# A first weight load given as 100 and 28 partitions, and a residual added ahead of the last products

## The chip, the cores and the metric

The kernel runs on one core of a Trainium2 chip. The metric is the device time of one execution in microseconds; before the change it is 196.32 us, the median of three runs (196.27 to 196.67). The core has five engines that run their own instruction streams and meet at semaphores: TensorE (PE in the profile, its weight loads PEld), VectorE (DVE), ScalarE (ACT), GpSimd (POOL) and SyncE (SP), which here issues nearly all of the transfers. Sixteen DMA engines move the data.

## The reference

One decoding step for 8 sequences: a layer of cached attention over the last 2,048 of 8,192 positions, then an MLP, each with a layer norm ahead of it and a residual.

```python
def _A_ref(x, k_cache, v_cache, wq, wo):          # x: 8 x 1 x 512
    q = (x @ wq)                                  # 32 heads of 128, 8 heads in the caches
    k, v = the last W = 2048 positions of the caches, each head used 4 times
    p = softmax(q k^T * Dh ** -0.5)
    return (p v) @ wo

def _B_ref(x, w1, w2, w3, w4):
    ...                                           # hs, from shifted parts of h
    x1 = x + hs
    h2 = gelu(layernorm(x1) @ w3) @ w4            # 512 -> 1792 -> 512
    return x1 + h2

x = A_x
h = x + _A_ref(layernorm(x), ...)
h2 = h + _B_ref(layernorm(h), ...)
return h2
```

With one position per sequence (S = 1) the shifted parts g0 to g3 are zero, so hs is zero and w1 and w2 are not needed. The result is h + layernorm(h) + gelu(layernorm(layernorm(h)) @ w3) @ w4. In this text "h's part" is h + layernorm(h).

## The kernel before, in words

The caches and the weights are some 79 MB, and the kernel streams them through on-chip memory once. SP issues all of these loads in one fixed order (`dma(SP, ...)`, line 187): wq, then the k and v blocks of 2 MB each into `ring`, a ring of eight buffers, then wo in four loads, w3 in one, and w4 in four. A load into a ring buffer waits until the products that read its former content are done; the first w4 load has such a wait (`w_free[1]`), the others follow it on SP without one. Each of the four w4 loads has a semaphore of its own (`sem_w4[0]` to `[3]`), and a load raises its semaphore by 16.

`B_w4` is 1,792 x 512. The loads take rows 0 to 511, 512 to 1023, 1024 to 1535 and 1536 to 1791; partition p of a load gets r neighbouring rows (r = 4, 4, 4, 2), which are 4,096 bytes (2,048 in the last load) that lie together in memory. So the first load is 128 partitions of 4,096 bytes. All loads of the stream have 128 partitions; x (`x_sb`, loaded at the start from ACT's queue) and the result have 8.

The attention part fills most of the time: transposes of k (L283), their copies to on-chip memory (L292, L294), scores (L303), softmax, products with v (L373). Behind it comes the tail, written out in a fixed order on each engine:

- `oR` (L414, L419) reorders the heads, `pe_wo` (L426) multiplies by wo into `hT_ps`.
- VectorE and TensorE make the sums for the layer norms (L512 to L526), `uT` among them. ScalarE takes two roots, `s2` (L542) and `s1` (L543); VectorE's reciprocal of `s2` is `r2` (L544).
- `pe_w3` (L536): 56 products in two parts, of 8 and 6 columns of the result, into `y_ps`. They need `uT` and w3.
- For each part VectorE multiplies by `r2` into `g_x` (L554), and ScalarE applies the gelu into `gT` (L556).
- Behind these on VectorE stands h's part: the reciprocal `r1` of `s1` (L557), `xb` (L558, L559), `fin` (L560), and its split into two bf16 halves, `f_hi` (L561) and `f_lo` (L562). The event at its end is `e_fin`.
- `pe_w4` (L568 through the helper `rows`): the products of `gT` with w4, in four chunks that go with the four loads, 16, 16, 16 and 8 matmuls, all added up in `z_ps`. Between the third chunk and the fourth, `pe_fin` (also L568) adds `f_hi` and `f_lo` by products with an identity, 8 matmuls.
- VectorE and ScalarE copy the four parts of `z_ps` out (L597, L595), and SP stores the result (L600).

An engine takes its instructions in the order in which the code lists them, and waits at an instruction whose semaphores have not come far enough.

Of the kernel before, what the change touches and what calls it, by code (L numbers as in the profile page):

```python
# [8 lines left out]
ALU = mybir.AluOpType  # L9
AX = mybir.AxisListType  # L10

B = 8
# [10 lines left out]
FC = F // 128  # L23
KC = D // 128
# [43 lines left out]
def bass_sequential_preLN__sliding_block_cached__mixer_s_mlp__decode_kernel(  # L68
# [23 lines left out]
    with es:  # L92
# [7 lines left out]
        ident_b = sb([128, 128], dt.bfloat16, "ident_b")  # L100
# [24 lines left out]
        w4_sb = ring[:, W4S, 0:FC * D].rearrange("p (k n) -> p k n", k=FC)  # L125
# [17 lines left out]
        NH = KC * B  # L143
        hp = sb([128, NH], dt.float32, "hp")
# [6 lines left out]
        hc = sb([128, NH], dt.float32, "hc")  # L151
# [3 lines left out]
        s1 = sb([128, B], dt.float32, "s1")  # L155
        s2 = sb([128, B], dt.float32, "s2")
        r1 = sb([128, B], dt.float32, "r1")
        r2 = sb([128, B], dt.float32, "r2")
        xb = sb([128, NH], dt.float32, "xb")
        fin = sb([128, NH], dt.float32, "fin")  # L160
# [3 lines left out]
        f_hi = sb([128, NH], dt.bfloat16, "f_hi")  # L164
        f_lo = sb([128, NH], dt.bfloat16, "f_lo")
# [14 lines left out]
        sem_wo = [S(f"sem_wo{i}") for i in range(NWO)]  # L180
        sem_x, sem_wq, sem_w3, sem_out = (S(n) for n in ("sem_x", "sem_wq", "sem_w3", "sem_out"))
        sem_w4 = [S(f"sem_w4{i}") for i in range(4)]
        PE, AC, DV, PO, SP = (Engine(S(n)) for n in ("s_pe", "s_act", "s_dve", "s_pool", "s_sp"))

        def dma(eng, dst, src, sem, *waits):
            def f(e):
                e.dma_start(dst, src).then_inc(sem, 16)  # L187
            eng.op(f, *waits, inc=False)
# [16 lines left out]
        e = DV.op(lambda e: e.bn_stats(st6[:, :], x_sb[:, :]), X)  # L205
        e = DV.op(lambda e: e.bn_aggr(mv[:, :], st6[:, :]), e)
        e = AC.op(lambda e: e.activation(rstd[:, :], mv[:, 1:2], ACT.Sqrt, bias=eps1[0:B, :], scale=1.0), e, e_eps)
        e = DV.op(lambda e: e.reciprocal(rstd[:, :], rstd[:, :]), e)
# [23 lines left out]
        e = PE.op(pe_xT, e_xln, e_idb)  # L232
# [35 lines left out]
        e_sp, e_max, e_mT, e_neg, e_negps, e_negc, e_exp, e_PT, e_pT, e_lsel, e_Lb, e_rL, e_scale = ({} for _ in range(13))  # L268
        NG = NB * 8
        LAST = NB - 1  # L270
# [114 lines left out]
        v3 = lambda t: t.rearrange("p (n b) -> p n b", b=B)  # L385
        vr = lambda t: t.rearrange("p (n b) -> p b n", b=B)

        def bc(t):
            a = t[:, :]
            return bass.AP(tensor=a.tensor, offset=a.offset, ap=[a.ap[0], [0, KC], [1, B]])  # L390

        hT_ps = S_ps[0]
# [90 lines left out]
        for l in loads:  # L483
            what, b, j = l
            if what == "wo":
                n, qh = b, QH // NWO
# [3 lines left out]
            n = place[l]  # L490
# [6 lines left out]
        w_free = [taken[quads[n - NS]] for n in (len(quads), len(quads) + 1)]  # L497
# [4 lines left out]
        w4_ends = []  # L502
        for (f0, r), sem in zip(w4_rows, sem_w4):
            lo = len(w4_chunks)
            for i in range(r):
                w4_chunks[lo + i] = slice(f0 + i, f0 + 128 * r, r)
            dma(SP, w4_sb[:, lo:lo + r, :].rearrange("p r n -> p (r n)"),
                B_w4[f0:f0 + 128 * r, :].rearrange("(p r) n -> p (r n)", r=r), sem, w_free[1] if lo == 0 else None)
            w4_ends.append(lo + r)
        assert len(w4_chunks) == FC  # L510

# [14 lines left out]
        e_hc = DV.op(lambda e: e.scalar_tensor_tensor(v3(hc[:, :]), bc(msum), -1.0 / D, v3(hd[:, :]),  # L526
                                                      ALU.mult, ALU.add))
# [14 lines left out]
        e = AC.op(lambda e: e.activation(s2[:, :], vsum[:, :], ACT.Sqrt, bias=eps2[:, :], scale=(1.0 + EPS) / D), e_vs)  # L542
        e1 = AC.op(lambda e: e.activation(s1[:, :], vsum[:, :], ACT.Sqrt, bias=eps1[:, :], scale=1.0 / D))  # L543
        e_r2 = DV.op(lambda e: e.reciprocal(r2[:, :], s2[:, :]), e)  # L544

        def bcf(t, n):
            a = t[:, :]
            return bass.AP(tensor=a.tensor, offset=a.offset, ap=[a.ap[0], [0, n], [1, B]])

        e_gT = []  # L550
        for n in range(2):
            fn = (FH, FC - FH)[n]
            cs = slice(n * FH * B, (n * FH + fn) * B)
            e = DV.op(lambda e, n=n, cs=cs, fn=fn: e.tensor_tensor(v3(g_x[:, cs]), v3(y_ps[n][:, 0:fn * B]), bcf(r2, fn),  # L554
                                                                   ALU.mult), e_y[n], e_r2)
            e_gT.append(AC.op(lambda e, cs=cs: e.activation(gT[:, cs], g_x[:, cs], ACT.Gelu_apprx_tanh), e))  # L556
        e = DV.op(lambda e: e.reciprocal(r1[:, :], s1[:, :]), e1)  # L557
        e = DV.op(lambda e: e.tensor_tensor(v3(xb[:, :]), v3(hc[:, :]), bc(r1), ALU.mult), e, e_hc)  # L558
        e = DV.op(lambda e: e.tensor_tensor(xb[:, :], xb[:, :], hp[:, :], ALU.add), e)  # L559
        e = DV.op(lambda e: e.tensor_tensor(fin[:, :], hT_ps[:, 0:NH], xb[:, :], ALU.add), e)  # L560
        e = DV.op(lambda e: e.tensor_copy(f_hi[:, :], fin[:, :]), e)  # L561
        e_fin = DV.op(lambda e: e.tensor_tensor(f_lo[:, :], fin[:, :], f_hi[:, :], ALU.subtract), e)  # L562

        z_ps = S_ps[1]

        def rows(e, w, rhs, start=False, stop=False):
            for nb in range(KC):
                ins = e.matmul(z_ps[32 * nb:32 * nb + B, 0:128], w[nb], rhs[nb], start=start, stop=stop,  # L568
                               tile_position=(0, 32 * nb), skip_group_check=True)
            return ins  # L570

        def pe_w4(lo, hi, *waits):
            def f(e):
                for fc in range(lo, hi):
                    ins = rows(e, [gT[:, fc * B:(fc + 1) * B]] * KC,
                               [w4_sb[:, fc, nb * 128:(nb + 1) * 128] for nb in range(KC)],
                               start=(fc == 0), stop=(fc == FC - 1))
                return ins
            return PE.op(f, *waits)

        def pe_fin(e):
            for part in (f_hi, f_lo):
                ins = rows(e, [part[:, nb * B:(nb + 1) * B] for nb in range(KC)], [ident_b[:, :]] * KC)
            return ins

        pe_w4(0, w4_ends[0], (sem_w4[0], 16), e_gT[0], e_exp[LAST])
        pe_w4(w4_ends[0], w4_ends[1], (sem_w4[1], 16))
        pe_w4(w4_ends[1], w4_ends[2], (sem_w4[2], 16), e_gT[1])
        PE.op(pe_fin, e_fin)
        e_z = pe_w4(w4_ends[2], w4_ends[3], (sem_w4[3], 16))  # L590
        zr, orow = [z_ps[32 * nb:32 * nb + B, 0:128] for nb in range(KC)], [out_sb[:, nb * 128:(nb + 1) * 128] for nb in range(KC)]
        e_out = []
# [45 lines left out]
```

## Time and profile before

| | before |
|---|---|
| time, median of three runs | 196.32 us |
| time of the profiled execution | 196.32 us |
| its span, first to last instruction | 194.5 us |
| TensorE busy (matmul) | 150.1 us, 77% |
| VectorE, ScalarE, GpSimd busy | 85.0, 79.9, 32.4 us |
| DMA | 79.57 MB, mean 409 GB/s |
| mean granted TensorE clock | 0.877; 0.50 from 175 us to the end |

The span is the time from the first to the last instruction that the profiler records; the execution is 1.8 us longer. "Busy" is the time of recorded instructions. In the views that follow, L and a number is a line of the kernel before, "<-" names what an engine waited for, and all times are microseconds from the start of the span unless they are marked ns.

### The profile page before, as it was taken

The numbers are of one execution on the slowest core, as the hardware profiler recorded it, in microseconds if no ns is written. First come the engines' busy times: TensorE is split into PE (matmuls) and PEld (weight loads), VectorE is DVE, ScalarE is ACT, GpSimd is POOL, SyncE is SP. The second block draws the span as 40 slices with busy tenths as digits, with TensorE's granted clock in tenths as the row PEclk, the third lists the DMA queues.
The fourth block names the chain that finished last, engine by engine and source line by source line (L and its number), as shares of the span: only waits on it lengthen the run. The fifth ranks groups of instructions, "written<-read, shape, count | busy, mean of one in ns | idle before, by whom it ended". The sixth has DMA issues, their size and how long they took to land.

```text
span 194.5 us, 6261 instructions
## 1 busy us (share of the span) xinstructions
PE 150.1 (77%) x2885; PEld 124.1 (64%) x2885; DVE 85.0 (44%) x209; ACT 79.9 (41%) x93; POOL 32.4 (17%) x39
## 2 busy tenths in 40 slices
PE   0027999978979992999579987998799893784563
PEld 0027877757758881888368866786678673684451
DVE  7501446556565443355415451545354536401033
ACT  5000577875845650456225642564454313000041
POOL 8000000070340250008000610071008000000000
PEclk9999999999999999699969997899999965555555
DMA  6999999999999999999999999999999999999970
GB/s 217 431 431 428 431 431 428 424 431 430 428 431 428 428 428 431 431 428 423 428 428 431 428 428 431 424 428 428 424 431 424 428 428 426 416 418 415 415 306 37
DMA packets 7001, 79.57 MB, mean 409 GB/s; under 512 B 688, under 2 KB 704, under 8 KB 2752
## 3 DMA queue, kind: packets, MB, share of 16 engines
q1 hardware_dynamic: 6960, 79.18, 96.2%
q8 instruction: 22, 0.36, 0.7%
q10 hardware_dynamic: 16, 0.01, 0.0%
q14 instruction: 3, 0.02, 0.0%
HBM read 79.18 MB, written 0.01 MB: 407 GB/s over the span
## 4 chain that ended last, share of the span: by engine, by line
DMA 57%; PE 35%; DVE 4%; SPq 1%; issue 1%; ACT 0%; DVEq 0%
DMA ring<-in_A_k_cache_dram 49%; PE kT_ps L283 16%; PE oT_ps L373 9%; DMA ring<-in_B_w_dram 8%; PE S_ps L303 5%; PE sm L348 2%; DVE P_sb L338 1%; DVE pT_sb L353 1%; SPq L187 1%; PE sm L361 1%; PE sm L326 1%; PE sm L316 1%; PE S_ps L568 1%; ACT P_sb L330 0%; DVE kT_sb L294 0%
## 5 line engine op out<-in xcount | busy, mean ns | idle before, releaser
L292 ACT ACTIVATE kT_sb<-kT_ps 128x1024 bf16<-128x1024 bf16 x64 | 65.4, 1024 | 73.2 <-PE kT_ps L283 72.6
L283 PE MATMUL kT_ps<-ident_p,ring 128*128 128x128 bf16 x1024 | 73.0, 229 | 12.5 <-DMA ring<-in_A_k_cache_dram 12.5
L283 PEld LDWEIGHTS kT_ps<-ident_p,ring 128*128 128x128 bf16 x1024 | 62.0, 103 | 26.7 <-DMA ring<-in_A_k_cache_dram 13.4
L294 DVE COPY kT_sb<-kT_ps 128x1024 bf16<-128x1024 bf16 x64 | 44.3, 692 | 66.4 <-PE kT_ps L283 66.4
L338 POOL TENSOR_TENSOR P_sb<-P_sb,mask_b 128x512 bf16<-128x512 bf16 x28 | 28.3, 1041 | 117.1 <-PE kT_ps L283 83.1
L373 PE MATMUL oT_ps<-pT_sb,ring 128*128 128x16 bf16 x1024 | 34.1, 172 | 3.9 <-DVE oT_all L382 3.9
L373 PEld LDWEIGHTS oT_ps<-pT_sb,ring 128*128 128x128 bf16 x1024 | 32.1, 100 | 6.1 <-issue 6.0
L303 PE MATMUL S_ps<-kT_sb,qwin 128*32 128x512 bf16 x256 | 27.0, 406 | 0.0
L353 DVE COPY pT_sb<-sm 128x512 bf16<-128x512 bf16 x32 | 13.4, 419 | 7.5 <-PE sm L348 7.5
L348 PE MATMUL sm<-ident_b,P_sb 128*128 128x128 bf16 x128 | 13.2, 230 | 3.9 <-DVE pT_sb L353 1.6
L348 PEld LDWEIGHTS sm<-ident_b,P_sb 128*128 128x128 bf16 x128 | 8.6, 101 | 6.2 <-issue 4.5
L542 ACT ACTIVATE s<-vsum,eps 128x8 f32<-128x8 f32 x1 | 0.3, 301 | 24.3 <-DVE vsum L525 24.3
L330 ACT ACTIVATE P_sb<-S_ps,negcol 128x512 bf16<-128x512 f32 x8 | 5.5, 688 | 7.8 <-DVE negcol L329 7.8
L303 PEld LDWEIGHTS S_ps<-kT_sb,qwin 128*32 128x32 bf16 x256 | 6.8, 93 | 3.0 <-issue 0.2
L238 PE MATMUL S_ps<-xlnT,wbig 128*128 128x8 bf16 x128 | 3.6, 168 | 5.2 <-DMA wbig<-in_A_wq_dram 5.2
L238 PEld LDWEIGHTS S_ps<-xlnT,wbig 128*128 128x128 bf16 x128 | 3.5, 104 | 5.2 <-issue 5.2
L227 PE MATMUL sm<-ident_b,xln_b 8*128 8x8 bf16 x4 | 0.3, 176 | 7.7 <-DVE xln_b L209 7.7
L312 DVE TENSOR_REDUCE mcol<-S_ps 128x1 f32<-128x512 f32 x8 | 5.5, 689 | 1.6 <-PE S_ps L303 1.5
L426 PE MATMUL S_ps<-oR,wbig 128*128 128x8 bf16 x128 | 4.0, 168 | 2.7 <-DMA wbig<-in_A_wo_dram 1.9
L426 PEld LDWEIGHTS S_ps<-oR,wbig 128*128 128x128 bf16 x128 | 3.7, 104 | 3.0 <-DMA wbig<-in_A_wo_dram 2.0
L227 PEld LDWEIGHTS sm<-ident_b,xln_b 8*128 8x128 bf16 x4 | 0.2, 118 | 7.7 <-DVE xln_b L209 7.7
L361 PE MATMUL sm<-lsel,ones_f 128*128 128x32 f32 x16 | 3.6, 314 | 1.3 <-DVE lsel L357 1.3
(87 smaller groups left out, 69.5 us busy)
## 6 DMA issues: line engine op xcount, KB each, us to landing
ring<-in_A_k_cache_dram SPq DMA_DIRECT2D x16, 2048.0 KB, 26.9
ring<-in_A_v_cache_dram SPq DMA_DIRECT2D x16, 2048.0 KB, 22.3
wbig<-in_A_wq_dram SPq DMA_DIRECT2D x1, 4096.0 KB, 12.3
wbig<-in_A_wo_dram SPq DMA_DIRECT2D x4, 1024.0 KB, 28.0
ring<-in_B_w_dram SPq DMA_DIRECT2D x1, 1792.0 KB, 27.0
ring<-in_B_w_dram SPq DMA_DIRECT2D x3, 512.0 KB, 15.4
ring<-in_B_w_dram SPq DMA_DIRECT2D x1, 256.0 KB, 15.2
x_sb<-in_A_x_dram ACTq DMA_DIRECT2D x1, 8.0 KB
```

What stands on the lines that cost most here:

```text
L238: ins = e.matmul(S_ps[0][:, h * B:(h + 1) * B], wq_v[:, kc, h * DH:(h + 1) * DH], xlnT[:, kc * B:(kc + 1) * B], start=(kc == 0), stop=(kc ...
L283: ins = e.matmul(kT_ps[i % 2][:, c * 128:(c + 1) * 128], ring[:, s, n * DH:(n + 1) * DH], ident_p[:, :], is_transpose=True)
L292: e_lo[i] = AC.op(lambda e: e.activation(kT_sb[:, i % NKT, 0:1024], kT_ps[i % 2][:, 0:1024], ACT.Copy), e_Tlo[i], e_QK.get(i - NKT))
L294: e_hi[i] = DV.op(lambda e: e.tensor_copy(kT_sb[:, i % NKT, 1024:2048], kT_ps[i % 2][:, 1024:2048]), e_Thi[i], e_QK.get(i - NKT))
L303: ins = e.matmul(S_ps[b % 2][32 * h:32 * (h + 1), :], qwin[:, b, 4 * j + h, w0:w0 + 32], kT_sb[:, i % NKT, :].rearrange("p (c h k) -> p h ...
L312: e_max[b] = DV.op(lambda e: e.tensor_reduce(mcol[:, :], S_ps[b % 2][:, :], AX.X, ALU.max), e_QK[8 * b + 7], e_mT.get(b - 1))
L338: e_sp[b, r] = eng.op(lambda e, r=r, pb=pb, mb=mb: e.tensor_tensor(P4_sb[:, 128 * r:128 * (r + 1), :], pb, mb, ALU.mult), e_exp[b], e_PT.g ...
L348: ins = e.matmul(pT_ps[:, x * 128:(x + 1) * 128], P4_sb[:, 32 * c:32 * (c + 1), :].rearrange("p k h -> p (k h)"), ident_b[:, :], is_transp ...
L353: e_pT[b, r] = DV.op(lambda e: e.tensor_copy(pT_sb[:, b % NB3, 4 * r:4 * (r + 1), :].rearrange("p c n -> p (c n)"), pT_ps[:, :]), e_PT[b, ...
L361: e_Lb[b] = PE.op(lambda e: e.matmul(sm[:, LB], ones_f[:, :], lsel[:, :], start=True, stop=True), e_lsel[b], e_pT[b, 3])
L373: ins = e.matmul(dst, ring[:, s, n * DH:(n + 1) * DH], pT_sb[:, b % NB3, c, :].rearrange("p (h c j r) -> p c j h r", h=4, c=4, j=2)[:, cq, j],
L426: ins = e.matmul(hT_ps[:, nb * B:(nb + 1) * B], wo_v[:, q, r, nb * 128:(nb + 1) * 128], oR[:, r, q * B:(q + 1) * B], start=(q == 0 and r = ...
```

## The change

The change has two parts.

The first w4 load becomes two loads on SP, one right after the other: partitions 0 to 99 (rows 0 to 399 of `B_w4`) and partitions 100 to 127 (rows 400 to 511). Every partition gets the same bytes as before. Both raise `sem_w4[0]`, so the first chunk of w4's products waits for 32 there. The description given with the change says of the split that lower-numbered DMA engines carry more of the load. The wait for the ring buffer stands on the first of the two.

h's part moves forward on two engines. On VectorE its six instructions stand right behind `r2`, ahead of both `g_x`. On TensorE its eight products come directly behind w3's and start the sum in `z_ps` (they carry `start`); the four chunks of w4 follow one another, and the last ends the sum. The number of products and of VectorE instructions is the same as before. The lines from the first insertion on have higher numbers in the changed kernel (L554 becomes L565, L557 to L562 become L550 to L555, L568 becomes L572).

```diff
+        P0 = 100
...
-            dma(SP, w4_sb[:, lo:lo + r, :].rearrange("p r n -> p (r n)"),
-                B_w4[f0:f0 + 128 * r, :].rearrange("(p r) n -> p (r n)", r=r), sem, w_free[1] if lo == 0 else None)
+            cuts = (0, P0, 128) if lo == 0 else (0, 128)
+            for p0, p1 in zip(cuts, cuts[1:]):
+                dma(SP, w4_sb[p0:p1, lo:lo + r, :].rearrange("p r n -> p (r n)"),
+                    B_w4[f0 + p0 * r:f0 + p1 * r, :].rearrange("(p r) n -> p (r n)", r=r), sem,
+                    w_free[1] if lo + p0 == 0 else None)
...
         e_r2 = DV.op(lambda e: e.reciprocal(r2[:, :], s2[:, :]), e)
+        e = DV.op(lambda e: e.reciprocal(r1[:, :], s1[:, :]), e1)
+        e = DV.op(... xb = hc * r1)
+        e = DV.op(... xb = xb + hp)
+        e = DV.op(... fin = hT_ps + xb)
+        e = DV.op(... f_hi = fin)
+        e_fin = DV.op(... f_lo = fin - f_hi)
...
-        (the same six lines, behind the loop over g_x and gT)
...
-                               start=(fc == 0), stop=(fc == FC - 1))
+                               stop=(fc == FC - 1))
...
-                ins = rows(e, [part[...] for nb in range(KC)], [ident_b[:, :]] * KC)
+                ins = rows(e, [part[...] for nb in range(KC)], [ident_b[:, :]] * KC,
+                           start=(part is f_hi))
...
-        pe_w4(0, w4_ends[0], (sem_w4[0], 16), e_gT[0], e_exp[LAST])
+        PE.op(pe_fin, e_fin, e_exp[LAST])
+        pe_w4(0, w4_ends[0], (sem_w4[0], 32), e_gT[0])
         pe_w4(w4_ends[0], w4_ends[1], (sem_w4[1], 16))
         pe_w4(w4_ends[1], w4_ends[2], (sem_w4[2], 16), e_gT[1])
-        PE.op(pe_fin, e_fin)
         e_z = pe_w4(w4_ends[2], w4_ends[3], (sem_w4[3], 16))
```

More of the change, by code (lines that the diff above doesn't have):

```diff
@@ L544, in bass_sequential_preLN__sliding_block_cached__mixer_s_mlp__decode_kernel @@
         e_r2 = DV.op(lambda e: e.reciprocal(r2[:, :], s2[:, :]), e)
+        e = DV.op(lambda e: e.reciprocal(r1[:, :], s1[:, :]), e1)
+        e = DV.op(lambda e: e.tensor_tensor(v3(xb[:, :]), v3(hc[:, :]), bc(r1), ALU.mult), e, e_hc)
+        e = DV.op(lambda e: e.tensor_tensor(xb[:, :], xb[:, :], hp[:, :], ALU.add), e)
+        e = DV.op(lambda e: e.tensor_tensor(fin[:, :], hT_ps[:, 0:NH], xb[:, :], ALU.add), e)
+        e = DV.op(lambda e: e.tensor_copy(f_hi[:, :], fin[:, :]), e)
+        e_fin = DV.op(lambda e: e.tensor_tensor(f_lo[:, :], fin[:, :], f_hi[:, :], ALU.subtract), e)
         def bcf(t, n):
@@ L556, in bass_sequential_preLN__sliding_block_cached__mixer_s_mlp__decode_kernel @@
             e_gT.append(AC.op(lambda e, cs=cs: e.activation(gT[:, cs], g_x[:, cs], ACT.Gelu_apprx_tanh), e))
[L557 to L562, printed above, removed]
         z_ps = S_ps[1]
@@ L582, in pe_fin @@
             for part in (f_hi, f_lo):
-                ins = rows(e, [part[:, nb * B:(nb + 1) * B] for nb in range(KC)], [ident_b[:, :]] * KC)
-            return ins
-        pe_w4(0, w4_ends[0], (sem_w4[0], 16), e_gT[0], e_exp[LAST])
+                ins = rows(e, [part[:, nb * B:(nb + 1) * B] for nb in range(KC)], [ident_b[:, :]] * KC,
+                           start=(part is f_hi))
+            return ins
+        PE.op(pe_fin, e_fin, e_exp[LAST])
+        pe_w4(0, w4_ends[0], (sem_w4[0], 32), e_gT[0])
         pe_w4(w4_ends[0], w4_ends[1], (sem_w4[1], 16))
         pe_w4(w4_ends[1], w4_ends[2], (sem_w4[2], 16), e_gT[1])
-        PE.op(pe_fin, e_fin)
         e_z = pe_w4(w4_ends[2], w4_ends[3], (sem_w4[3], 16))
```

## The prediction

> **What bounds the kernel now.** First the chain of waits from 184 us to the end, because both edits lie there. Its columns are start, duration and what the end waited for.
>
> ```profile
> 175.54 15.42 DMA ring<-in_B_w_dram
> 190.96 0.04 issue
> 191.00 1.05 PE S_ps L568 x32
> ...
> 192.08 0.28 DVE out_sb L597
> ```
>
> The end hangs on the weight loads, then on the last products of w4 (L568), then on the copy out. So an edit pays only as far as it brings forward the last landing of w4 or shortens the products behind it.
>
> Second, the activity by stretches of half a microsecond. The last two columns are the share of the 16 DMA engines that is busy and GB/s.
>
> ```profile
> 186.00:186.50 0.50, 0.00 (x0) 0.00 (x0) 0.39 (x3) 0.14 (x1) 0.00 (x0) 0.50 1.02 412
> 187.00:187.50 0.50, 0.15 (x5) 0.18 (x6) 0.00 (x0) 0.50 (x1) 0.00 (x0) 0.50 0.66 270
> 189.00:189.50 0.50, 0.50 (x23) 0.48 (x24) 0.17 (x2) 0.10 (x1) 0.00 (x0) 0.50 0.51 205
> 190.50:191.00 0.50, 0.00 (x0) 0.00 (x0) 0.24 (x2) 0.00 (x0) 0.00 (x0) 0.50 0.32 123
> ```
>
> Until 186.5 all engines move rows; at 187.2 two thirds do, at 189.2 half, at 190.7 five of sixteen. Every load gives every engine the same number of rows, yet the engines do not finish together. The sixteen increments that the last w4 load leaves in the trace say how far apart they are: six at 186.95 to 187.23, one each at 187.88 and 188.75, three at 189.89 to 190.11, five at 191.24 to 191.59. The kernel waits for these five.
>
> Third, what sets them back: the DMA queues (packets, MB, share of 16 engines).
>
> ```profile
> q1 hardware_dynamic: 6960, 79.18, 96.2%
> q8 instruction: 22, 0.36, 0.7%
> ```
>
> The 22 instruction fetches of 16 KB run on the same engines. On one engine the packet records follow each other without a gap (the next starts some 4 ns before the last one's recorded end), so the records can be strung into sixteen chains. The fetch at 18.55 us took 0.94 us, and the row behind it 1.10 us in place of 0.61, so its engine lost 0.93 + 0.49 = 1.42 us for good. The chains show the fetches going round eight engines in turn: 22 = 8 + 8 + 6, the last (189.6 us) too late to hold up more than an increment. So five engines lose three fetches (187.1 + 4.26 = 191.4, found 191.24 to 191.59) and three lose two (187.1 + 2.84 = 189.9, found 189.89 to 190.11).
>
> Which five? The load of x_sb has 8 partitions, 8 packets, and 8 of the chains carry one; I take these for the lower-numbered half. Where two chains run within 3 ns of each other they can be swapped, but by the best fit the turn goes over six engines of the upper half, then two of the lower, and the late five are the first five. If a turn goes over consecutive numbers upwards, that is 10 to 15, then 0 and 1, and the late five are 10 to 14. The trace has no engine numbers, and this step is the weakest.
>
> Last, the timeline behind w3's landing (187.21), which says what TensorE and VectorE must do meanwhile.
>
> ```profile
> 186.70 0.20 DVE L544 RECIPROCAL r<-s 128x8 f32<-128x8 f32 x1 [0.28 <-ACT s L542]
> 187.35 1.95 PE L536 MATMUL kT_ps<-uT,ring 128*128 128x8 bf16 x56 [1.72 <-DMA ring<-in_B_w_dram]
> 188.58 0.23 DVE L554 TENSOR_TENSOR g_x<-kT_ps,r 128x64 f32<-128x64 f32 x1 [1.68 <-PE kT_ps L536]
> 189.22 0.33 PEld L568 LDWEIGHTS S_ps<-ring,gT 128*8 128x8 bf16 x16
> 189.45 0.19 DVE L557 RECIPROCAL r<-s 128x8 f32<-128x8 f32 x1
> 190.58 0.19 DVE L562 TENSOR_TENSOR f_lo<-fin,f_hi 128x32 bf16<-128x32 f32 x1
> 191.00 0.60 PE L568 MATMUL S_ps<-ring,gT 128*8 128x128 bf16 x16 [0.70 <-DMA ring<-in_B_w_dram]
> 191.39 0.32 PE L568 MATMUL S_ps<-ident_b,f_hi 128*8 128x128 bf16 x4
> 191.63 0.40 PE L568 MATMUL S_ps<-ring,gT 128*8 128x128 bf16 x8
> ```
>
> VectorE idles 1.68 us while w3's products run; TensorE idles from about 190.3 to 191.0 for the third w4 load.
>
> **The split load.** A w4 row of 4,096 bytes follows the last after 155 ns on an engine (the first increments of the first two loads, 183.81 and 185.07, are 1.26 us apart for 8 rows and an increment). The loads seen share rows equally: 128 partitions as 8 rows on each of 16 engines, 8 as one row on each of 8. An equal share of 100 over at most 16 engines means 10 engines with 10 rows, of 28 it means 14 with 2. If the lower-numbered are taken, as the change says, engines 0 to 9 carry 12 rows in place of 8, 10 to 13 carry 2, and 14 and 15 none. [...]
>
> The sum for each group, by its last increment: engines 10 to 13, 191.24 to 191.59 less 6 x 0.155 = 0.93, so 190.31 to 190.66. Engine 14: less 1.24, at most 190.35. Engine 15: about 188.9. Engines 0 and 1: 189.90 plus 4 x 0.155 = 0.62, so 190.52. The rest: at most 188.75 + 0.62 = 189.37. The last landing moves from 191.59 to about 190.66, 0.93 us earlier. The third load moves as much, 190.96 to 190.03. w3 stands ahead of w4 in each engine's queue and stays at 187.21.
>
> The cost of issuing: one DMA more on SP, 0.47 to 0.60 us by the shorter issues of the trace. Behind it stand the other w4 loads and, much later, the store. SP finishes issuing at 179.07, and no engine's first w4 load ends before 183.81, so this hides; without that cover it would be those 0.5 us. The first wait of w4's products asks for 32 in place of 16, so for both parts: with the numbers above it is met at 187.5, before they can start.
>
> Unknown is whether rows in blocks of ten per engine are as fast as the old share. The nearest row is the store, 8 partitions at once: its 1,024-byte packets took 44 to 91 ns. So a row may cost anything from 155 ns to about twice that; below 155 ns no row has been seen. I take 155, since the three kinds of load with 128 partitions all run at one even rate, and keep the other end.
>
> **h's part.** Six VectorE instructions (L557 to L562, 189.45 to 190.77, 1.32 us) move ahead of g_x. They can start when r2 is done (186.90; s1 is ready at 186.85) and end at 188.22, and g_x starts at 188.58 when w3's first products are out: hidden with 0.36 us to spare. Without that cover, the first gelu and all w4 products would wait up to 1.32 us. On TensorE eight products (191.39 to 191.63, 0.24 us) move from the third gap between w4's chunks to behind w3's. There they delay w4's first products from 189.22 to 189.46. Sixteen products take 0.39 us (191.00 to 191.39), so three chunks end at 189.46 + 1.17 = 190.63, and the last chunk waits for its load until 190.66 + 0.04 = 190.70. Nothing is queued on TensorE behind these eight but w4. Left in place, they would start when f_lo is ready, 190.81, and end at 191.05: the move is worth 0.35 of the gain, and nothing without the earlier loads.
>
> **Sum.** The last chunk starts at 190.70 in place of 191.63, 0.93 us earlier; the tail behind it (copies, store) is unchanged. The profiled execution took 196.32 us with a span of 194.5, and 196.32 is also the median of the three runs: 196.32 - 0.93 = 195.39. More than 1.0 us is not to be had, since TensorE is then the bound (190.63).
>
> **Rivals.**
> *A late engine is among the ten (slower).* If the turn runs downwards, or starts elsewhere in another execution, one of the late engines carries 12 rows: 191.24 to 191.59 plus 0.62, so 0.27 to 0.62 us longer, 196.6 to 196.9. It decides as soon as one engine with three fetches is below 10. For it: no numbers in the trace, and 8 and 9 are of the upper half too. Against: six turns in the upper half and then two in the lower fit an upward count that wraps after 15. 15%.
> *Rows in blocks of ten are slow.* Doubled, the ten rows cost 1.55 us more on engines 0 and 1: 190.52 + 1.55 = 192.07, 0.5 us longer, 196.8. It eats gain from 0.14 us on and makes the kernel slower from 1.07 us. For it: the store's 91 ns. Against: these two engines run nearly 3 us behind most of the others, which have then left the same stretch. 11%: 3 in 100 still faster (about 195.8), 3 the same, 5 slower.
> *The parts go over all sixteen engines evenly, so nothing moves.* Then the five stay at 191.59, h's products have left a gap in which TensorE waits anyway, and the time is 196.3. [...] Against it: 100 has no equal share over 16. 6%.
>
> **How the numbers follow.** The forecast, 195.39 with its own range 195.2 to 195.7 (gain 1.0 at most and the 0.05 by which the runs go below the median; at the other end a third of a microsecond lost to slower rows or increments), has 68%. Below 195.2 TensorE forbids. With the partly slow rows and the even split, 195.2 to 196.5 holds 68 + 6 + 6 = 80%; the slower cases, 196.6 to 196.9, are left out. A measurement here can tell 0.2%, 0.39 us, from no change: faster 0.68 + 0.03 = 0.71, same 0.03 + 0.06 = 0.09, slower 0.15 + 0.05 = 0.20.
>
> **What would show it.** Right: five late increments near 190.3 to 190.66 with two more beside them; the DMA share still above 0.5 at 189.5 and near zero at 190.7; xb to f_lo between 186.9 and 188.3; h's products before w4's; the wait ahead of the last chunk nearly gone. Wrong: a last increment past 191.6 (a late engine was given more), g_x later than 188.6, or a first load that ends after 189.4.

## The result and the profile after

The changed kernel takes 199.56 us, median of six runs (199.06 to 200.39), against 196.68 us for the kernel before in the runs beside it (six runs, 196.27 to 198.98). The ratio is 1.0146, with a 95% interval of 1.0115 to 1.0176: 2.9 us slower, where 0.93 us less was forecast. The profiled execution took 199.06 us with a span of 197.3.

The chain of waits from 184 us on (start, duration, what the end waited for; "issue" is time for which the profile shows no wait):

```profile
184.00 0.35 PE S_ps L427 x13
184.35 4.04 issue
188.39 0.23 PE S_ps L427 x2
...
189.79 0.19 DVE uT L523
...
192.71 0.40 ACT gT L567 x2
...
193.11 1.69 PE S_ps L572 x44
...
194.83 0.28 DVE out_sb L602
```

The chain no longer names a weight load, but this reading is close to a tie. `uT` was ready at 189.98, and the last increment of w3's load came at 190.23; w3's products began at 190.36, which is 0.13 us after the landing, as before (187.21 and 187.35). The chain follows one of two nearly equal causes. The activity by stretches shows the other (last two columns: share of the DMA engines busy, GB/s):

```profile
183.00:183.50 0.50, 0.50 (x25) 0.50 (x23) 0.00 (x0) 0.00 (x0) 0.00 (x0) 0.50 1.12 258
186.00:186.50 0.50, 0.00 (x0) 0.00 (x0) 0.00 (x0) 0.00 (x0) 0.00 (x0) 0.50 0.98 291
187.00:187.50 0.50, 0.00 (x0) 0.00 (x0) 0.00 (x0) 0.00 (x0) 0.00 (x0) 0.50 0.91 268
189.00:189.50 0.50, 0.50 (x3) 0.50 (x4) 0.06 (x1) 0.00 (x0) 0.00 (x0) 0.50 1.01 215
193.00:193.50 0.50, 0.39 (x18) 0.42 (x22) 0.00 (x0) 0.10 (x1) 0.00 (x0) 0.50 0.13 49
```

The kernel before, in the same stretch:

```profile
183.00:184.00 1.00, 0.84 (x30) 0.76 (x29) 0.00 (x0) 0.00 (x0) 0.00 (x0) 0.50 1.03 414
```

The first of the five lines is the one to look for: at 183 us all engines are busy and move 258 GB/s, where the kernel before moved 414 with all engines busy. The engines are not idle, they are slow. The packet records say it row by row: w3's rows of 3,584 bytes take 140 ns until 182 us and a median of 250 to 284 ns between 183 and 185; rows of 4,096 bytes take a median of 159 ns until 183 us and of 268 to 334 between 183 and 186, 216 to 274 up to 190. From 191 on they take 159 again. In the kernel before no w4 row of 4,096 bytes took more than 159 ns, and of w3's 512 rows three took more than 140, one behind the other right after an instruction fetch. The slow stretch begins when the first engines reach the cut load (w3's first increment came at 182.69, the first slow row began at 182.84), and it covers engines that are still at w3, whose increments run on to 190.23.

The first cut load raised its semaphore by 24 single increments and two early ones, which fits 10 engines for the 100 partitions and 14 for the 28, as forecast. The rest did not follow:

| us | before | after |
|---|---|---|
| last increment of w3 | 187.21 | 190.23 |
| w3's products begin | 187.35 | 190.36 |
| last increments of the four w4 loads | 188.42, 189.66, 190.96, 191.59 | 191.26, 192.25, 193.47, 194.09 |
| the copies out begin | 192.08 | 194.83 |

The timeline of the tail:

```profile
190.36 1.95 PE L540 MATMUL kT_ps<-uT,ring 128*128 128x8 bf16 x56 [0.41 <-DVE msq L526]
191.21 1.28 ACT L567 ACT_TABLE_LOAD   x1
192.35 0.19 DVE L555 TENSOR_TENSOR f_lo<-fin,f_hi 128x32 bf16<-128x32 f32 x1
192.46 0.33 DVE L565 TENSOR_TENSOR g_x<-kT_ps,r 128x64 f32<-128x64 f32 x2
192.71 0.39 ACT L567 ACTIVATE gT<-g_x 128x64 bf16<-128x64 f32 x2 [0.22 <-DVE g_x L565]
193.11 1.66 PE L572 MATMUL S_ps<-ring,gT 128*8 128x128 bf16 x56
```

The cover for h's part is gone too: g_x comes right behind f_lo, not behind w3's first products. It costs little, since ScalarE's table load ends at 192.49 and the gelu starts at 192.71: 0.22 us.

### The profile page after: what moved, and what is told of

It is laid out like the page before. It is cut to its first block, busy times and chain, and to the rows that moved or that the text cites. A ratio compares the mean times of both kernels' runs of the same rounds, so it can differ in the third digit from the quotient of the medians.

```text
span 197.3 us, 6262 instructions
## 1 busy us (share of the span) xinstructions
PE 150.7 (76%) x2885; PEld 125.1 (63%) x2885; DVE 84.8 (43%) x209; ACT 79.7 (40%) x93; POOL 32.3 (16%) x39
## 4 chain that ended last, share of the span: by engine, by line
DMA 49%; PE 39%; DVE 6%; issue 4%; ACT 1%; SPq 0%; DVEq 0%
DMA ring<-in_A_k_cache_dram 49%; PE kT_ps L284 17%; PE oT_ps L374 9%; PE S_ps L304 5%; PE sm L349 2%; PE S_ps L427 2%; DVE P_sb L339 1%; DVE pT_sb L354 1%; PE sm L362 1%; PE S_ps L572 1%; PE sm L327 1%; PE sm L317 1%; DVE oT_all L383 0%; SPq L188 0%; ACT P_sb L331 0%
## 5 line engine op out<-in xcount | busy, mean ns | idle before, releaser
L284 PE MATMUL kT_ps<-ident_p,ring 128*128 128x128 bf16 x1024 | 73.9, 230 | 14.0 <-DMA ring<-in_A_k_cache_dram 14.0
L284 PEld LDWEIGHTS kT_ps<-ident_p,ring 128*128 128x128 bf16 x1024 | 62.8, 103 | 28.7 <-DMA ring<-in_A_k_cache_dram 15.0
```

What stands on the lines that cost most here:

```text
L284: ins = e.matmul(kT_ps[i % 2][:, c * 128:(c + 1) * 128], ring[:, s, n * DH:(n + 1) * DH], ident_p[:, :], is_transpose=True)
```

## The experiments

Three theories stood at the start, guesses of the author that the runs were to decide between. *Path*: in a load of 128 partitions every engine writes partitions that no other engine writes; in a load of fewer neighbouring partitions engines share the way to the same partitions, and everything that goes there slows. *Late engine*: only the number of rows on the engines that are behind counts. *Move*: h's part ahead of g_x is the loss. Ratios are to the kernel before, run beside each experiment, with 95% intervals.

**The cut alone.**

```diff
 # the kernel before, with
+            cuts = (0, 100, 128) if lo == 0 else (0, 128)
 # and 32 in the first chunk's wait
```

> The load as 100 and 28 partitions, h's part left in its old place. Path theory (the 100-partition load makes the DMA engines' rows slow for all): rows of 4,096 bytes take 230 to 330 ns in place of 159 from the first row of this load on, the last w4 increment lands near 194, and the time is 198.5 to 200, as with the whole change. Late-engine theory (only the number of rows on the late engines counts): rows stay at 159 ns, last increment at 191.9 to 192.3, time 196.7 to 197.3. Move theory (the slower time comes from h's part ahead of g_x): no loss, 196.3 to 196.7.

Measured: 199.55 us, ratio 1.0151 (1.0124 to 1.0177). Last w4 increment 195.08. This trace also settles the tie. Here `uT` was ready at 187.45 and TensorE still waited for w3's rows, which landed at 189.96:

```profile
190.09 1.94 PE L539 MATMUL kT_ps<-uT,ring 128*128 128x8 bf16 x56 [2.67 <-DMA ring<-in_B_w_dram]
```

The chain of waits of this trace, from 182 us on, names the weight loads up to 194.47:

```profile
177.51 16.96 DMA ring<-in_B_w_dram
194.47 0.04 issue
194.52 1.05 PE S_ps L571 x32
```

The cut by itself is the whole loss, and the late landings are how it acts. The long stall of TensorE in the profile after is not needed for it: here the stall at the same place is 1.55 us.

**The move alone.**

```diff
 # the changed kernel, with
-            cuts = (0, P0, 128) if lo == 0 else (0, 128)
+            cuts = (0, 128)
 # and 16 in the first chunk's wait
```

> One first load of 128 partitions, h's part moved. Path theory: rows at 159 ns, last increment at 191.6 as before, and the time within 0.2 us of before. Move theory: g_x late by up to 0.9 us and the time 197 to 199.5.

Measured: 196.44 us, ratio 0.9994 (0.9976 to 1.0012); last increment 191.45, rows at 159 ns. No difference that can be told. The move theory falls. In this execution g_x was again held by h's part:

```profile
187.68 1.98 PE L540 MATMUL kT_ps<-uT,ring 128*128 128x8 bf16 x56
188.85 1.28 ACT L567 ACT_TABLE_LOAD   x1
190.00 0.19 DVE L555 TENSOR_TENSOR f_lo<-fin,f_hi 128x32 bf16<-128x32 f32 x1
190.11 0.33 DVE L565 TENSOR_TENSOR g_x<-kT_ps,r 128x64 f32<-128x64 f32 x2
190.36 0.39 ACT L567 ACTIVATE gT<-g_x 128x64 bf16<-128x64 f32 x2 [0.23 <-DVE g_x L565]
```

The table load ends at 190.13, so the gelu lost 0.23 us.

**A cut with equal shares, 96 and 32, and one of 64 and 64.** Both are the changed kernel with another P0.

```diff
-        P0 = 100
+        P0 = 96      # and, in the other kernel, 64
```

> Cuts at 96 in place of 100: both parts can be shared equally by sixteen engines (6 and 2 rows each), so every engine keeps 8 rows, but no engine's block of rows is one of the old ones. Path theory, if the blocks are at fault: rows above 200 ns while the 96-partition part runs and the last increment later than 192; time 197.5 to 200. Late-engine theory (unequal numbers are at fault): rows at 159 ns, last increment 191.6, time as before.

> Cuts at 64: 4 rows on each engine from either part. If a block of four neighbouring partitions is what suits the engines, rows stay at 159 ns or nearly so, last increment 191.6, time as before. If any load of fewer than 128 partitions disturbs, rows above 200 ns and a time over 197.5.

Measured: 198.97 us, ratio 1.0127 (1.0101 to 1.0153), and 199.77 us, ratio 1.0154 (1.0128 to 1.0181). The first load raised its semaphore by 32 single increments in either, 16 for each part, so every engine has its 8 rows; and both lose about as much as the cut at 100. The late-engine theory falls as the cause. So does the guess that blocks of four neighbouring partitions suit the engines. The activity of the 64 and 64 kernel:

```profile
183.00:184.00 1.00, 0.73 (x28) 0.65 (x25) 0.00 (x0) 0.00 (x0) 0.00 (x0) 0.50 1.07 249
184.00:185.00 1.00, 0.00 (x0) 0.00 (x0) 0.00 (x0) 0.00 (x0) 0.00 (x0) 0.50 0.99 268
```

Two sequels were open: that any second load on the semaphore disturbs, or that it is the smaller number of partitions.

**Two loads, cut by columns.**

```diff
+            halves = 2 if lo == 0 else 1
+            c = r * D // halves
+            for j in range(halves):
+                dma(SP, w4_sb[:, lo:lo + r, :]...[:, j * c:(j + 1) * c], ...)   # all 128 partitions
```

> The first w4 load as two loads again, but cut by columns: each has all 128 partitions and half of their bytes. Path theory (in a load of 128 partitions every engine writes partitions that no other engine writes; a load of fewer makes engines share the way to the same partitions): rows of 2,048 bytes at 84 ns, rows of 4,096 at 159, last increment at 191.6 to 191.7, time within 0.3 us of before. Rival (two loads on one semaphore, or simply one load more in the queue, is what disturbs): rows slow as in the other cuts, time over 198.

Measured: 196.34 us, ratio 0.9991 (0.9975 to 1.0008); rows of 2,048 bytes at 84 ns and of 4,096 at 159, last increment 191.63.

```profile
183.00:184.00 1.00, 0.89 (x30) 0.81 (x30) 0.00 (x0) 0.00 (x0) 0.00 (x0) 0.50 1.04 410
184.00:185.00 1.00, 0.00 (x0) 0.00 (x0) 0.00 (x0) 0.00 (x0) 0.00 (x0) 0.50 1.03 408
```

One load more, and one semaphore for two, cost nothing that can be told. It is the cut by partitions.

**Half the first load, in one piece or in eight.** The upper 64 partitions of the first load are left out in both. The lower 64 come by one load, or by eight loads of 8 partitions with a step of 4.

```diff
+            parts = [slice(0, 64)] if lo == 0 else [slice(0, 128)]
 # or
+            parts = [slice(b + o, b + 32, 4) for b in (0, 32) for o in range(4)] if lo == 0 else [slice(0, 128)]
+            for j, ps in enumerate(parts):
+                dma(SP, w4_sb[ps, lo:lo + r, :]..., B_w4[...][ps, :], sem, ...)
 # and 16, or 128, in the first chunk's wait
```

> The upper 64 partitions of the first w4 load are left out; the lower 64 come by one load, 4 rows on each of 16 engines. Path theory: sixteen engines write where only eight wrote before, so rows slow to 230 ns and more while this load runs, though it moves half as many bytes; w3's last increment later than 188.5. Source theory (reading the weights' rows is what clashes): the same for this one.

> [...] Path theory: every row stays at 159 ns (140 for w3), w3's last increment at 187.2 as before. Source theory, or a cost of any load under 128 partitions: rows over 200 ns again.

Measured, one run each, so the rows count here and not the times: 197.56 us in one piece, 195.73 in eight. In one piece w4's rows between 183 and 184 us had a median of 216 ns, somewhat less than the 230 that was expected, w3's 196 with a longest of 296, and w3's last increment came at 188.64. In eight pieces the rows stayed at 159 and 140 (but for one beside a fetch), last increment of w4 190.62. The source theory falls with these. w3's last increment came at 187.55, 0.34 after that of before (187.21). The eight loads did not set it back: the last increment of the third wo load, before any row of w4 moved, was already 0.40 late (180.73 against 180.33).

The step of 4 was the author's choice under the path theory, meant to keep each engine to partitions of its own. No trace shows that it does so, and no other step was tried. What the runs show is the rows: 159 ns against 216 in this pair, 159 against 302 in the next.

**The same eight loads, written to the upper half.** Source rows, sizes and number of loads are the same; only the destination differs. The lower half of the first load is left out and the upper gets the wrong rows; the kernel that writes the lower half was run beside it.

```diff
+                dst = slice(ps.start + 64, ps.stop + 64, 4) if lo == 0 else ps
-                dma(SP, w4_sb[ps, lo:lo + r, :]...
+                dma(SP, w4_sb[dst, lo:lo + r, :]...
```

> The same eight loads of 8 partitions with a step of 4, with the same rows of w4 as source, but written to partitions 64 to 127: only the destination differs from the kernel that writes the lower half. The lower 64 partitions of the first load are left out and the upper ones get the wrong rows. Path theory: the eight engines that carry these loads now write where the other eight write w3, so rows of both slow to 230 ns and more (w3's to 200 and more), w3's last increment comes after 188, and the time is 1 to 2 us over that of the lower-half kernel. Source theory (which rows are read, by how many engines) or a plain cost of small loads: no difference between the two, rows at 159 and 140 ns.

> The kernel with eight loads to partitions 0 to 63 once more, timed beside the one that writes the upper half; the upper 64 partitions of the first load are left out. Path theory and source theory both: 195.5 to 196.2, rows at 159 and 140 ns.

Measured: upper half 198.63 us, ratio 1.0105 (1.0082 to 1.0128); lower half 196.81 us, ratio 0.9999 (0.9978 to 1.0020). The stretches of the upper one, then of the lower one:

```profile
183.00:184.00 1.00, 0.70 (x27) 0.61 (x23) 0.00 (x0) 0.00 (x0) 0.00 (x0) 0.50 1.09 224
184.00:185.00 1.00, 0.25 (x3) 0.17 (x3) 0.25 (x2) 0.00 (x0) 0.00 (x0) 0.50 0.99 227
```

```profile
183.00:184.00 1.00, 0.87 (x30) 0.78 (x30) 0.00 (x0) 0.00 (x0) 0.00 (x0) 0.50 1.05 418
184.00:185.00 1.00, 0.00 (x0) 0.00 (x0) 0.00 (x0) 0.00 (x0) 0.00 (x0) 0.50 1.05 415
```

With the upper half as the destination, w4's rows took 302 ns in place of 159 and w3's 278 in place of 140 in the microsecond from 183, and w3's last increment came at 189.03 in place of 187.23. Twice 159 is 318 and twice 140 is 280: rows of both loads went at about half their rate. The path theory reads this so: the engines still at w3 were writing to the upper half, and rows slow where two engines are on the way to the same partitions. The runs show the times and the destination. TensorE waits for these rows, with its stall ahead of wo's last products only 0.76 us long:

```profile
189.16 1.95 PE L541 MATMUL kT_ps<-uT,ring 128*128 128x8 bf16 x56 [3.14 <-DMA ring<-in_B_w_dram]
```

The lower kernel's time did not come down to the 195.5 to 196.2 that was expected, though its last increment was early in the profile (191.40): there TensorE had a stall of 2.25 us and was late (`uT` at 187.71 against 185.65 before), so its own chain set the end.

**The cut on the last load.**

```diff
-            cuts = (0, P0, 128) if lo == 0 else (0, 128)
+            cuts = (0, P0, 128) if r == 2 else (0, 128)
 # and 16 in the first chunk's wait, 32 in the last's
```

> Full result; the cut into 100 and 28 partitions is on the last w4 load (2,048-byte rows) in place of the first; h's part moved. Path theory: only what is in flight beside these rows suffers, so w3's last increment is at 187.2 to 188.2, the 2,048-byte rows take 130 to 240 ns while the first engines carry them and the loss is 0.3 to 1.5 us, well under the 2.9 of the cut in the first load. If the loss came from the number of rows on late engines alone: last increment 191.6 minus 0.5 to plus 0.3, no loss over 0.3 us.

Measured: 197.13 us, ratio 1.0025 (1.0007 to 1.0044), 0.5 us. Rows of 2,048 bytes took a median of 120 ns between 187 and 188 (84 before; 130 to 240 had been expected), w3 landed at 187.94, the last increment came at 192.24. So a cut slows what is in flight beside it; with the cut in the first load, 183 of w3's 512 rows took more than 140 ns and 285 of w4's 384 rows of 4,096 bytes more than 160 in the profile after. That the slow rows made the 0.5 us is not shown: in this trace TensorE's own chain set the end, with `uT` at 188.04, after w3's landing.

**Fewer bytes for the upper half.** The way to unload the late engines that the path theory leaves: put the last 256 rows of w4 wholly on partitions 0 to 63, and load them in eight pieces with the step of 4.

```diff
-FC = F // 128
+FC = F // 128 + 2
-        w4_rows, ... = ((0, 4), (512, 4), (1024, 4), (1536, 2)), {}
+        w4_rows, ... = ((0, 4, 128), (512, 4, 128), (1024, 4, 128), (1536, 4, 64)), {}
...
 # the last four chunks use gT[0:64, ...] and w4_sb[0:64, ...]; 16 in the first wait, 128 in the last
 # the second kernel: the same in the kernel before
```

> Full result; h's part moved; the first three w4 loads of 128 partitions, and the last 256 rows of w4 all on partitions 0 to 63 (4 rows each, products over 64 partitions), loaded as eight loads of 8 partitions with a step of 4. Path theory: rows at 159 ns; the upper-half engines have 0.65 us less to carry, so their last increment is near 190.9, the lower-half ones 0.6 us more, 190.5 at most; TensorE has 16 products more and is then the bound; 0.3 to 0.6 us faster than before. If a load under 128 partitions disturbs in any form: 198 to 200.

> Full result; the last 256 rows of w4 on partitions 0 to 63 by eight loads with a step of 4, as before, but h's part in its old place: behind both g_x on VectorE, and its products ahead of the last chunk. If h's part ahead of g_x is what the other such kernel lost (g_x 1 us late in its trace): g_x follows w3's first products within 0.1 us, 196.2 to 196.8, level with the kernel before or 0.3 us faster. If the 16 products more on TensorE are what costs: 197.0 to 197.6, as with h's part moved.

Measured: 197.38 us, ratio 1.0041 (1.0025 to 1.0057), with h's part moved, and 197.34 us, ratio 1.0030 (1.0013 to 1.0047), with h's part in its old place. For the first, 0.3 to 0.6 us less had been forecast; the second fits the branch in which the products cost. On the side of the loads the first did what was forecast, but for one engine: rows at 159 ns, the late engines of the upper half done with their last load at 190.66 to 190.80, and one lower engine, held by the last instruction fetch, at 191.48 in place of 190.5 at most. On TensorE it lost more than that:

```profile
183.78 2.54 issue
...
187.97 2.82 PE kT_ps L541 x64
190.80 1.71 PE S_ps L573 x45
```

w3's products take 2.82 us in place of 1.95, and TensorE was late for them (`uT` at 187.93). Their number rose only from 56 to 64; the sixteen that give 64 columns are the slow ones, 60 ns from one start to the next where the others take 33, in both kernels:

```profile
L541 PE MATMUL kT_ps<-uT,ring 128*128 128x8 bf16 x48 | 1.8, 175 | 0.1
L541 PE MATMUL kT_ps<-uT,ring 128*64 128x8 bf16 x16 | 1.1, 202 | 0.0
```

With h's part back, g_x started a microsecond earlier (189.38 against 190.40) but the gelu waited for the table load until 190.55 (190.66 with the move), so the place of h's part decides nothing here either. No version with the full result beat the kernel before.

## Why the prediction was wrong

**The step that failed** is the price of a row in the cut load: "I take 155, since the three kinds of load with 128 partitions all run at one even rate, and keep the other end". In place of 155 ns, rows of 4,096 bytes took a median of 268 to 334 between 183 and 186 us. All loads in the stream of before have 128 partitions, and their even rate does not go with every load: the eight small loads kept 159 ns in the lower half and took 302 in the upper. So a price from 128 partitions could not be carried over to 100. The store's 44 to 91 ns was the nearest row for few partitions; what slows its slower packets, no run shows. The rival built on it was given 11%.

**The upper bound was placed on too few rows.** The rival doubled the ten rows of engines 0 and 1 alone and came to 196.8. The runs show that rows of other loads, on other engines, slow as well: w3's from 140 to 250 and more. "w3 stands ahead of w4 in each engine's queue and stays at 187.21" was the false sentence in it. That w3 is issued first does not keep its rows clear of the cut load: early engines reach the cut load while late ones are still at w3 (its increments came from 182.69 to 190.23), and between 184 and 185 the rows of both took a median of 284 and 334 ns. w3's last increment moved by 3.02 us, the copies out by 2.75, the median by 2.88.

**The rival of an even split** had the parts spread over all sixteen engines, and so nothing gained and nothing lost: 196.3. The cuts at 96 and at 64 did spread so, with 16 single increments for each part, and cost 1.27% and 1.54%. Leaving the load whole was the right decision, but the price of a cut is not nothing. What bore on it was the rate: the 64 and 64 cut fell to 249 GB/s with all engines busy, the cut by columns kept 410.

**The late engines.** The 24 increments that came one by one fit engines that carry rows, ten and fourteen, as forecast. That the ten are the lowest-numbered no run shows, since the traces have no engine numbers. But the second w4 load gave its first increment at 184.98 and its next at 187.69. The early one had at most two rows of the cut load and no fetch to catch up, so one of the six engines outside the ten was not late, and the turn over 10 to 15, 0 and 1 was a wrong guess. With late engines among the ten, this rival would have cost up to 0.6 us by itself; it was not tried alone, since every cut into blocks of partitions that was run slowed the rows as well. It is not needed: the cut at 64, with equal shares, lost as much.

**What held.** The wait on w4's last increments as the bound before, the 22 fetches of 1.42 us as what sets five engines back, the even share of rows, and SP's extra issue, which is hidden (its last load was issued by 177.8). The gain of 0.35 from the move was to come only with the earlier loads, and those did not come.

**A smaller miss.** h's part ahead of g_x was held to be hidden with 0.36 us to spare, and it was not. The sum took TensorE's progress from one trace, in which `uT` was ready well ahead of w3 (185.65 against 187.21). Where `uT` comes later, w3's first products are out before f_lo: with the move alone `uT` came at 187.62, after w3's landing at 187.07. It cost 0.22 us in the profile after and 0.23 with the move alone.

**What stays open.** The runs show rows at about half the rate when only the destination changes and the source rows stay (302 ns against 159, 278 against 140), and no loss that can be told from one load more (ratio 0.9991 with the cut by columns) or from eight small loads in the lower half (0.9999). That it is engines on the same group of partitions which halve each other's rate is the author's reading; no trace names the partitions that an engine writes. How far a slow row on one engine holds up rows to partitions that nobody shares is not separated.

**TensorE's stall** stands ahead of the last two products with wo: 0.22 us before, 4.04 in the profile after. The traces point to an instruction fetch. In all fourteen, these two products start 1.26 to 1.59 us after the end of the last instruction fetch but one; in the profile after that fetch began at 185.65 in place of 181.71 and took 1.24 us in place of 0.96. Of these 3.9 us, 2.7 were there a fetch earlier (177.73 against 175.00), before any row was slow; at most the rest comes from the cut. The stall does not set the loss: it was 2.30 us with the move alone and 2.25 in the lower-half kernel, which lost nothing that can be told, and 1.55 with the cut alone and 0.76 in the upper-half kernel, which lost 1.5% and 1.05%. What sets the time of a fetch stays open.

## What to carry to other kernels

While other loads are in flight, cut a load by columns and not into blocks of neighbouring partitions: here every such cut slowed what ran beside it (rows of 159 ns to a median of 268 to 334 with the cut at 100), and the cut by columns did not (159). Eight loads of 8 partitions with a step of 4 did not in the lower half (159), and did in the upper (302). The author's guess from this, which no run tried alone, is that an engine that is behind is not relieved by giving its partitions to another engine while both are at work; fewer bytes for partitions 64 to 127 did bring the late engines in earlier (190.80 in place of 191.59), at a price on TensorE (2.82 us for w3's products in place of 1.95). Before a price from the trace is used for a new shape, ask what the rows that it comes from have in common: here it was all 128 partitions.

## What the runs showed of the hardware

- Busy is not moving: the share of busy DMA engines stayed at 0.96 to 1.07 while the rate fell from over 400 to between 204 and 300 GB/s (184 to 188 us of the profile after). Share and GB/s have to be read together.
- Eight small loads written to partitions 64 to 127 in place of 0 to 63: 302 ns a row against 159, and 278 against 140 for w3's rows beside them, nearly the double.
- The loads of 100 and 28 partitions gave 24 single increments, which fits 10 and 14 engines; two early ones (173.28 and 175.61, while SP was issuing the load) must hold the other 8 of the 32 that the first chunk waits for.
- An instruction fetch of 16 KB took 0.88 to 1.05 us of one DMA engine in the trace of before, and beside rows of 16 KB set its data back by 1.42 us; by the packet chains of that trace eight engines take the 22 fetches in turn, and the ends of equal shares lie 4.6 us apart (186.95 to 191.59).
- TensorE's stall, of 0.22 to 4.04 us, ended in all fourteen traces 1.26 to 1.59 us after the end of the same instruction fetch; the author's reading is that a fetch that comes late in the data queues holds TensorE up.
- In the two kernels with fewer bytes for the upper half, w3's products of 128 columns followed each other after 33 ns, those of 64 columns after 60.
